# Loading k, q and v of the second step over the POOL queue, in one line with the weights

## The chip, the cores and the metric

The kernel runs on one core of a Trainium2 chip. The metric is the device time of one execution in microseconds (us); lower is better.

## The reference

There are two parts, one after the other. The first is gated linear attention with 4 batches, 8 heads, 768 positions and head size 48: with f = sigmoid(f_logit), at each position the 48 x 48 state of a head becomes `f * state + outer(k, v)`, and the output is `q @ state`. The second takes x, the outputs in rows of 8 x 48 = 384 (3072 rows), through a feed-forward net (FFN):

```
out = (relu(x @ w_gate) * (x @ w_val)) @ w_out     # 384 -> 1536 -> 384
```

Inputs and output are float32.

## The kernel before

**Steps and work items.** The sequence is cut into 6 steps of 128 positions. A work item is one step of one batch (all 8 heads, 4 pairs of heads), so there are 24. For an item, f goes through exp and ln on ACT, is summed along the step by a matmul with a triangle (L583; step 0: L482), and gives decay factors; k and q are multiplied with them into `hats` (L603, L606 on POOL; step 0: L509 on POOL for k and on DVE for q); TensorE transposes these (L616; step 0: L519), forms scores (L639), DVE masks them (L645), and TensorE forms the outputs from the scores and v (L667 for step 0, L678 later) and from the state (L674). The state is advanced by L719 and the lines after it. POOL casts v to bf16 into `vpad` first (L559). The outputs go as `xT` to the FFN.

**FFN.** `ffn_hidden` forms one of 12 slices of 128 hidden columns: a gate and a value matmul group (L767), relu on ACT (L774), and the product on DVE (L778). `ffn_out` multiplies the 12 slices with `wo` (L790), ACT copies the result out (L810), SP stores it (L813). For step 0 the hidden groups run in the order: slices 0 to 3 of batches 0 and 1, the same slices of batches 2 and 3, then slices 4 to 7 of batches 0 and 1, and so on; a chain named "ffn" keeps them in that order on TensorE.

**Loads.** Each load of f, k, q or v takes one batch (step 0) or two batches (384 KB, later steps). It is cut in runs of 192 bytes, 2048 of them for two batches; f, k and q of step 0 use runs of 384 bytes. SP issues all of these in one line (L400). The weights are float32 in memory and are cast to bf16 by the DMA; POOL issues them in one line (L420), in three slices each: wg0, wv0 to wg2, wv2, and wo0 to wo2. The list `early` gives the order for steps 0 and 1. Buffers of the inputs are three deep (`NL`).

**How two queues are kept apart.** In `early`, an item of one queue is tied to an item of the other that is `lag` planned microseconds of transfer behind it. For SP's loads this is a true dependency (a wait for the landing). For a weight it is `paced`, except for the three slices of wo, which truly wait for the landing of f, k and q of step 1 (`wo_after`).

**The plan.** `Plan.schedule` runs all operations through a model of the five engines and of the DMA (`occ`, `lat`, `prio`, `flow`, `late`), always taking the operation that can start first; ties go to the lower `prio`. The order found is the program order of each engine. `Plan.needs` then emits the waits, and leaves out two kinds of ties:

```
                if how in ("order", "pace"):
                    continue
```

So a paced operation has its place in the program order, worked out with planned times, but no wait on the chip. While TensorE would be idle in the plan before the first FFN group, it gets matmuls on zeros (L456). The first FFN group ends these.

Of the kernel before, what the change touches and what calls it, by code (L numbers as in the profile page):

```python
# [8 lines left out]
BF16 = mybir.dt.bfloat16  # L9
# [34 lines left out]
class Plan:  # L44
# [4 lines left out]
    def __init__(self, limits):  # L49
        self.ops = []  # L50
        self.limits = limits
        self.settled, self.margin = 0.0, {}

# [41 lines left out]
    def schedule(self, banks):  # L95
# [14 lines left out]
        left = len(self.ops)  # L110
        flow_free = 0.0

# [8 lines left out]
        while left:  # L121
# [17 lines left out]
            e = op.eng  # L139
# [14 lines left out]
            if op.flow is not None:  # L154
                backlog = max(flow_free - op.end, 0.0)
                flow_free = op.end + backlog + op.flow
                op.end += op.flow + op.late + (min(backlog, op.flow) if op.ring == "own" else backlog)
            free[e] = at + op.occ
# [70 lines left out]
def bass_hgrn2_outer__then__ffn_reglu_kernel(  # L229
# [12 lines left out]
             "q0.2.3 q0.3.4 v0.2.3 v0.3.4 wg0 wv0 wg1 wv1 wg2 wv2 f1.0.2 k1.0.2 q1.0.2 v1.0.2 wo0 wo1 "  # L242
             "wo2 f1.2.4 k1.2.4 q1.2.4 v1.2.4").split()
    lag = 4.0
    first_xbar_qk = 4
    flight = 3
    WP = 0
# [5 lines left out]
    n_tiled = 1  # L253
    first_xbar_x = 3
    load_batches = 2
    hat_engines = ['DVE', 'POOL']
    STORE = 'SP'
    TAIL = [0, 256, 384]
    groups = [(0,0,4,1),(1,0,2,0),(1,2,4,0),(2,0,4,0),(3,0,4,0),(4,0,4,0),(5,0,4,0)]
    B, H, S, D = q.shape  # L260
    C = 128
# [8 lines left out]

    VSTEP, SSTEP = 112, 96
    VW, SW = NP * VSTEP, NP * SSTEP
# [16 lines left out]
    NV = 4  # L289
    vpad = [sb(f"vpad{i}", [128, VW], BF16) for i in range(NV)]  # L290
    st = [[sb(f"st{b}_{i}", [128, SW], BF16) for i in range(2)] for b in range(B)]
# [28 lines left out]
    pl = Plan({"bc": 1, "tp": 1, "s": 4, "y": 1, "kv": 1, "f": 4, "w": 1})  # L320
    pl.settled, pl.margin = 40.0, {"PE": 0.5, "SP": 0.6}
    add = pl.add
    gp, ve, sc, te, sy = nc.gpsimd, nc.vector, nc.scalar, nc.tensor, nc.sync
# [41 lines left out]
    for i in range(NH):  # L365
        zero("DVE", ve, hats[i][:], f"hats{i}", 1024, -8)
    for i in range(NV):
        zero("POOL", gp, vpad[i][:], f"vpad{i}", VW, -7)
    for i in range(NA):
# [14 lines left out]
    srcs = {"f": f_logit, "k": k, "q": q, "v": v}  # L384

    def load(n, c, b0, b1, after=(), paced=(), eng="SP"):
        last = tails.get("load" + eng)
        e = sy if eng == "SP" else sc
        t = ld[n][c % NL]
        src = bass.AP(tensor=srcs[n].tensor, offset=b0 * H * S * D + c * C * D,  # L390
                      ap=[[D, C], [S * D, (b1 - b0) * H], [1, D]])
        dst = t[:, b0:b1, :, :].rearrange("p b h d -> p (b h) d")
        flow = 1.0 * (b1 - b0)
        if c == 0 and n != "v":
            u = b0 % 2
            src = bass.AP(tensor=srcs[n].tensor, offset=b0 * H * S * D, ap=[[2 * D, 64], [S * D, H], [1, 2 * D]])
            dst = t[64 * u:64 * u + 64, b0 - u:b0 - u + 2, :, :].rearrange("p b h d -> p (b h d)").rearrange(
                "p (h x) -> p h x", h=H)
            flow = 0.82
        op = add(eng, lambda: e.dma_start(dst, src), [], [f"{n}{c % NL}_{b}" for b in range(b0, b1)],  # L400
                 occ=(0.8 if eng == "SP" else 0.3) * (b1 - b0) * (0.8 if c == 0 else 1), lat=2.0 if c == 0 else 0.9, prio=c * 100 - 150 * (eng != "SP"), after=after,
                 follows=[last] if last else [], paced=paced)
        tails["load" + eng] = op
        dma(op, f"{n}{c % NL}_{b0}{b1}", flow, (6.0 if (c, n, b0) == (1, "v", 0) else 2.0) if c else 0.8)
        return op
# [4 lines left out]
    def load_w(nm, s, after, landed=()):  # L410
        if nm == "wo":
            src = bass.AP(tensor=w_out.tensor, offset=s * WJ * 128 * DM,
                          ap=[[DM, 128], [128 * DM, WJ], [1, DM]])
            dst = wo[:, s * WJ:(s + 1) * WJ, :]
        else:
            src = bass.AP(tensor=wsrc[nm].tensor, offset=s * WJ * 128,
                          ap=[[DFF, 128], [128 * DFF, NK], [1, WJ * 128]])
            dst = (wg if nm == "wg" else wv)[:, :, s * WJ * 128:(s + 1) * WJ * 128]
        last = tails.get("load_w")
        op = add("POOL", lambda: gp.dma_start(dst, src), [], [f"{nm}{s}"], occ=0.8, lat=1.0, prio=WP, paced=after,  # L420
                 after=landed, follows=[last] if last else [])
        tails["load_w"] = op
        dma(op, f"{nm}{s}", 6.3 / wsteps)
        return op


    done, first_of = [], {}
    wo_after = ['f', 'k', 'q']
    for item in early:
        weight = item[0] == "w"  # L430
        cost, need = 0.0, []
        for other, flow, op in reversed(done):
# [3 lines left out]
            cost += flow  # L436
        if weight:
            landed = [first_of[wo_after[int(item[2:])]]] if item[:2] == "wo" else []
            op = load_w(item[:2], int(item[2:]), [] if landed else need, landed)
# [107 lines left out]
    def attention(c, b):  # L547
# [5 lines left out]
        xi = c % NX  # L553
        fin, kin, qin, vin = (ld[n][li] for n in "fkqv")

        qk_key = [f"qkT{qi}_0", f"qkT{qi}_1"]
        vp = vpad[vi]
        vout = bass.AP(tensor=vp, offset=0, ap=[[VW, 128], [VSTEP, NP], [64, 2], [1, D]])
        add("POOL", lambda: gp.tensor_copy(vout, vin[:, b, :, :].rearrange("p (n j) d -> p n j d", j=2)), [f"v{li}_{b}", f"vpad{vi}"], [f"v_{vi}"],  # L559
            prio=P + 3, occ=0.15 + HD / 1200.0 * 1.1, lat=0.2)  # L560
# [7 lines left out]
        else:  # L568
# [27 lines left out]
            if c < NC - 1:  # L596
# [11 lines left out]
                [f"q{li}_{b}", f"expq{ei}", f"hats{hi}"], [f"hq{hi}"], prio=P + 2, occ=0.95, lat=0.2)  # L608
            if c < first_xbar_qk:
                tp = Bank("tp")  # L610
# [71 lines left out]
        if c < n_tiled:  # L682
            chain("intra", "PE", intra, qk_key + [f"v_{vi}", f"vpad{vi}", f"ptm{mi}_0", f"ptm{mi}_1"]
                  + (s_key if c else []), [y], occ=0.1 + (0.8 if c else 0.5), lat=PE_L, prio=P + 7, opens=[y])
# [3 lines left out]
        else:  # L688
# [4 lines left out]
                **act_t(HD))  # L693
            if c < first_xbar_x:
                xp = Bank("tp")
# [17 lines left out]
        if c < NC - 1:  # L713
# [3 lines left out]
            def state():  # L717
                for p in range(NP):
                    mm = te.matmul(kv.ap[:, p * 96:(p + 1) * 96],  # L719
                                   khat[:, p * 128:(p + 1) * 128],  # L720
                                   bass.AP(tensor=vp, offset=p * VSTEP, ap=[[VW, 128], [64, 2], [1, D]]))
                return mm
# [58 lines left out]
    def ffn_out(g, *bs):  # L781
# [26 lines left out]
        for b, n0, n1, o in parts:  # L808
# [6 lines left out]
            dma(op, f"osb{oi}_{n0}", 0.45 * (n1 - n0) / DM)  # L815

    first_stores = [tails["loadSP"]] if '0' == "1" else []
    OJ = 4
# [3 lines left out]
    pend = []  # L822
    loads = [op for weight, flow, op in done if not weight]
    len0 = 0
    for c in range(NC):
        for b in range(0, B, load_batches):
            for n in "fkqv":
                if c > max(int(x.split(".")[0]) for x in sent):
                    if load_engine == "SP":
# [105 lines left out]
```

## Time and profile before

| | us |
|---|---|
| median of 3 runs | 198.84 (198.35 to 201.0) |
| the profiled execution | 199.44 |
| its span in the profile | 197.3 |
| PE busy in it | 190.8 |
| DVE, ACT, POOL busy | 108.9, 115.9, 77.1 |

The profile is of one execution. PE is TensorE's matmuls, PEld its weight loads, POOL is GpSimd, SP the engine that issues most DMAs; a trailing q means an engine's queue of instructions. A line such as `24.60 0.41 PE L667 MATMUL ... x16` gives start, duration, engine, source line and how many instructions were merged; a bracket at its end tells how long the engine was idle before it and what ended that. The trace also has a record of each DMA packet with its queue, size, start and duration; where packet rates or landings are given, they are counted from these records (a landing is the last of the 16 semaphore packets that end a DMA).

### The profile page before, as it was taken

How to read it: one execution, taken by the hardware profiler on the slowest of the kernel's cores; microseconds unless marked ns; L12 is line 12 of the kernel's file. 1: busy time of each engine (PE TensorE's matmuls, PEld its weight loads, DVE VectorE, ACT ScalarE, POOL GpSimd, SP SyncE). 2: the span in 40 equal slices, each digit the busy share in tenths (PEclk: the TensorE clock that was granted, in tenths of full speed). 3: DMA queues.
4: the chain of work that ended last, by engine and by line, in shares of the span. 5: the costliest groups of instructions: out<-in, count | busy, mean ns of one | idle time of the engine just before them, and what ended most of it. 6: DMA issues, size and time to landing. Idle time of an engine off the chain costs nothing.

```text
span 197.3 us, 4555 instructions
## 1 busy us (share of the span) xinstructions
PE 190.8 (97%) x1804; PEld 125.5 (64%) x1819; DVE 108.9 (55%) x212; ACT 115.9 (59%) x264; POOL 77.1 (39%) x111
## 2 busy tenths in 40 slices
PE   7999899988999999999999999999999999999995
PEld 5777688856788687866565555554554555544564
DVE  7269675575098959586956562832645433442300
ACT  2975866905879495868668577386334433344312
POOL 5188302553567593949483744604500000000000
PEclk9999999999999999999999999999999999999999
DMA  4999999999998999899997996988951310111113
GB/s 122 234 224 193 181 212 204 201 207 234 250 240 177 195 196 204 176 194 199 133 205 155 232 186 138 203 194 170 150 133 40 47 50 26 40 43 40 40 40 120
DMA packets 114100, 30.70 MB, mean 156 GB/s; under 512 B 107040, under 2 KB 114080, under 8 KB 114080
## 3 DMA queue, kind: packets, MB, share of 16 engines
q1 hardware_dynamic: 110096, 26.88, 67.6%
q0 software_dynamic: 3984, 3.54, 11.6%
q8 instruction: 14, 0.23, 0.5%
q14 instruction: 6, 0.05, 0.1%
HBM read 25.95 MB, written 4.72 MB: 155 GB/s over the span
## 4 chain that ended last, share of the span: by engine, by line
PE 82%; DMA 6%; ACT 3%; SPq 2%; DVE 2%; POOL 2%; issue 1%
PE ps L767 43%; PE ps L790 23%; DMA wo<-in_moe_w_out_dram 4%; PE ps L639 3%; DMA q_in<-in_q_dram 2%; SPq L400 2%; PE ps L616 2%; PE ps L678 2%; PE ps L719 2%; PE ps L674 2%; PE ps L456 1%; PE ps L583 1%; ACT relu L774 1%; PE ps L519 1%; DVE hats L509 1%
## 5 line engine op out<-in xcount | busy, mean ns | idle before, releaser
L778 DVE TENSOR_TENSOR gT<-relu,ps 128x256 bf16<-128x256 bf16 (+1 forms) x96 | 52.1, 551 | 61.7 <-PE ps L767 40.9
L767 PE MATMUL ps<-xT,wv 128*128 128x256 bf16 (+1 forms) x285 | 61.8, 325 | 0.2
L774 ACT ACTIVATE relu<-ps 128x256 bf16<-128x256 f32 (+1 forms) x96 | 46.4, 491 | 25.4 <-PE ps L767 24.4
L767 PE MATMUL ps<-xT,wg 128*128 128x256 bf16 (+1 forms) x276 | 59.9, 323 | 0.5
L790 PE MATMUL ps<-wo,gT 128*128 128x384 bf16 (+2 forms) x300 | 52.2, 319 | 1.2 <-DMA wo<-in_moe_w_out_dram 1.2
L790 PEld LDWEIGHTS ps<-wo,gT 128*128 128x128 bf16 x300 | 27.9, 98 | 19.2 <-DMA wo<-in_moe_w_out_dram 1.6
L767 PEld LDWEIGHTS ps<-xT,wv 128*128 128x128 bf16 x288 | 26.7, 98 | 16.1
L767 PEld LDWEIGHTS ps<-xT,wg 128*128 128x128 bf16 x288 | 26.6, 98 | 14.8
L645 DVE TENSOR_TENSOR ptm<-ps,tri 128x512 bf16<-128x512 f32 x48 | 30.5, 683 | 4.4 <-PE ps L639 4.2
L810 ACT ACTIVATE osb<-ps 128x384 f32<-128x384 f32 (+2 forms) x25 | 11.8, 477 | 32.9 <-PE ps L790 32.9
L603 POOL TENSOR_TENSOR hats<-k_in,expo 128x384 bf16<-128x384 f32 x20 | 20.0, 998 | 20.9 <-ACT expo L592 20.9
L735 POOL TENSOR_TENSOR st<-ssum,dec 128x384 bf16<-128x384 f32 x16 | 13.2, 829 | 21.5 <-DVE ssum L733 21.4
L606 POOL TENSOR_TENSOR hats<-q_in,expo 128x384 bf16<-128x384 f32 x20 | 19.9, 1000 | 2.0 <-DMA q_in<-in_q_dram 2.0
L456 PE MATMUL ps<-zeros 128*128 128x256 bf16 x91 | 14.2, 316 | 1.1 <-DVE zeros L360 1.1
L592 ACT ACTIVATE expo<-ps 128x384 f32<-128x384 f32 x20 | 9.8, 490 | 9.0 <-PE ps L585 7.3
L559 POOL CAST vpad<-v_in 128x384 bf16<-128x384 f32 x24 | 11.9, 512 | 1.9 <-DMA v_in<-in_v_dram 1.2
L692 ACT ACTIVATE xn<-ps 128x384 bf16<-128x384 f32 x20 | 9.9, 495 | 3.9 <-PE ps L678 3.9
L456 PEld LDWEIGHTS ps<-zeros 128*128 128x128 bf16 x91 | 9.8, 113 | 3.4 <-DVE zeros L360 1.1
L733 DVE TENSOR_TENSOR ssum<-ps,st 128x384 f32<-128x384 f32 x16 | 8.8, 549 | 2.8 <-PE ps L719 2.8
L594 ACT ACTIVATE expo<-ps 128x384 f32<-128x384 f32 x20 | 9.9, 497 | 0.0
L639 PE MATMUL ps<-qkT 48*128 48x128 bf16 x192 | 8.5, 218 | 0.6 <-ACT qkT L529 0.5
L639 PEld LDWEIGHTS ps<-qkT 48*128 48x128 bf16 x192 | 5.4, 94 | 5.0 <-issue 3.1
(71 smaller groups left out, 162.0 us busy)
## 6 DMA issues: line engine op xcount, KB each, us to landing
out_dram<-osb SPq DMA_DIRECT2D x23, 192.0 KB, 2.1
f_in<-in_f_logit_dram SPq DMA_DIRECT2D x10, 384.0 KB, 6.4
k_in<-in_k_dram SPq DMA_DIRECT2D x10, 384.0 KB, 5.5
q_in<-in_q_dram SPq DMA_DIRECT2D x10, 384.0 KB, 4.1
v_in<-in_v_dram SPq DMA_DIRECT2D x10, 384.0 KB, 5.3
wg<-in_moe_w_gate_dram POOLq DMA_DIRECT2D x3, 384.0 KB, 7.4
wv<-in_moe_w_val_dram POOLq DMA_DIRECT2D x3, 384.0 KB, 7.4
wo<-in_moe_w_out_dram POOLq DMA_DIRECT2D x3, 384.0 KB, 7.4
```

The source lines that it names most:

```text
L456: op = add("PE", lambda: te.matmul(cold.ap[:, 0:256], zeros[:, 0:128], zeros[:, :]), ["zeros"], [cold], occ=0.22 if i < 17 else 0.11, lat= ...
L559: add("POOL", lambda: gp.tensor_copy(vout, vin[:, b, :, :].rearrange("p (n j) d -> p n j d", j=2)), [f"v{li}_{b}", f"vpad{vi}"], [f"v_{vi} ...
L603: add("POOL", lambda: gp.tensor_tensor(hk, kin[:, b, :, :], ex[:, 1, :].rearrange("p (h d) -> p h d", h=H), ALU.mult), [f"k{li}_{b}", f"ex ...
L606: add("POOL", lambda: gp.tensor_tensor(hq, qin[:, b, :, :], ex[:, 0, :].rearrange("p (h d) -> p h d", h=H), ALU.mult), [f"q{li}_{b}", f"ex ...
L639: mm = te.matmul(s.ap[:, p * C:(p + 1) * C], qkT[qi][lo:lo + D, 1, p, :], qkT[qi][lo:lo + D, 0, p, :])
L645: add("DVE", lambda j=j, s=s: ve.tensor_tensor(ptm[mi][:, j, :, :], s.ap[:, :].rearrange("p (n t) -> p n t", n=NP), mask, ALU.mult), [s, " ...
L735: add("POOL", lambda: gp.tensor_tensor(t4(s_new), t4(tmp), rate, ALU.mult), [key] + dk, [f"S{b}_{c % 2}"], prio=P + 8, **pool_t(HD))
L767: mm = te.matmul(bank.ap[:, 0:n], wt[:, kt, j * 128:(j + 1) * 128], xT[xi][:, kt, n0:n1], start=(kt == 0), stop=(kt == NK - 1))
L774: add("ACT", lambda: sc.activation(relu[ri][:, 0:n], gate.ap[:, 0:n], AF.Relu), [gate], [f"relu{ri}"], prio=P, **act_t(n))
L778: add("DVE", lambda: ve.tensor_tensor(gT[gi][:, j, n0:n1], relu[ri][:, 0:n], val.ap[:, 0:n], ALU.mult), [val, f"relu{ri}"], [f"gT{gi}_{j}_ ...
L790: mm = te.matmul(o.ap[:, 0:n1 - n0], gT[gi][:, j, b * C:(b + 1) * C], wo[:, j, n0:n1], start=(j == 0), stop=(j == NJ - 1))
L810: add("ACT", lambda o=o, oi=oi, n0=n0, n1=n1: sc.activation(osb[oi][:, n0:n1], o.ap[:, 0:n1 - n0], AF.Copy), [o], [f"osb{oi}_{x}" for x in ...
```

## The change

The loads of k, q and v of step 1 are issued by POOL instead of SP, in one chain ("soft") with the weights. They are paced and have no wait. f of step 1 stays on SP, with a true tie as before. The slices of wo lose their waits and are paced like the other weights. `lag` becomes 6, and in `early` wo2 moves behind k of batches 2 and 3. The plan's model has two DMA flows, SP's and POOL's, that slow each other, in the place of one. `vpad` becomes one tensor with a pitch of 128 columns for a pair of heads instead of 112, zeroed by one memset of the gaps. Two thresholds count work items instead of steps. The core of the diff:

```diff
     early = ("f0.0.1 f0.1.2 f0.2.3 f0.3.4 k0.0.1 k0.1.2 q0.0.1 q0.1.2 v0.0.1 v0.1.2 k0.2.3 k0.3.4 "
              "q0.2.3 q0.3.4 v0.2.3 v0.3.4 wg0 wv0 wg1 wv1 wg2 wv2 f1.0.2 k1.0.2 q1.0.2 v1.0.2 wo0 wo1 "
-             "wo2 f1.2.4 k1.2.4 q1.2.4 v1.2.4").split()
-    lag = 4.0
-    first_xbar_qk = 4
+             "f1.2.4 k1.2.4 wo2 q1.2.4 v1.2.4").split()
+    lag = 6.0
+    first_xbar_qk = 16
...
-    first_xbar_x = 3
+    first_xbar_x = 12
...
+    SOFT = {1: "kqv"}
...
             if op.flow is not None:
-                backlog = max(flow_free - op.end, 0.0)
-                flow_free = op.end + backlog + op.flow
-                op.end += op.flow + op.late + (min(backlog, op.flow) if op.ring == "own" else backlog)
+                me, you = ("POOL", "SP") if e == "POOL" else ("SP", "POOL")
+                backlog = max(flow_free[me] - op.end, 0.0)
+                shared = min(max(flow_free[you] - op.end - backlog, 0.0), op.flow * self.share[me])
+                flow_free[me] = op.end + backlog + op.flow + shared
+                flow_free[you] += min(shared, op.flow) if shared else 0.0
+                op.end += op.flow + op.late + backlog + shared
...
+    pl.share = {"SP": 2.0, "POOL": 0.4}
...
-    for i in range(NV):
-        zero("POOL", gp, vpad[i][:], f"vpad{i}", VW, -7)
+    add("POOL", lambda: gp.memset(vpad[:, 0:B, :].rearrange("p b (h x) -> p (b h) x", x=64)[:, :, D:64], 0.0), [], ["vpad"],
+        occ=0.6, prio=-7)
...
+    def load_soft(n, c, b0, b1, paced):
+
+        last = tails.get("soft")
+        t = ld[n][c % NL]
+        src = bass.AP(tensor=srcs[n].tensor, offset=b0 * H * S * D + c * C * D, ap=[[D, C], [S * D, (b1 - b0) * H], [1, D]])
+        dst = t[:, b0:b1, :, :].rearrange("p b h d -> p (b h) d")
+        op = add("POOL", lambda: gp.dma_start(dst, src), [], [f"{n}{c % NL}_{b}" for b in range(b0, b1)],
+                 occ=1.25, lat=1.0, prio=WP + c * 160 - 160, paced=paced, follows=[last] if last else [])
+        tails["soft"] = op
+        dma(op, f"s{n}{c % NL}_{b0}{b1}", 0.75 * (b1 - b0), 2.0)
...
     def load(n, c, b0, b1, after=(), paced=(), eng="SP"):
+        if n in SOFT.get(c, ""):
+            return load_soft(n, c, b0, b1, list(after) + list(paced))
...
-        last = tails.get("load_w")
+        last = tails.get("soft")
...
-    wo_after = ['f', 'k', 'q']
+    wo_after = ['none']
     for item in early:
-        weight = item[0] == "w"
+        weight = item[0] == "w" or item[0] in SOFT.get(int(item[1]), "")
...
-        if weight:
-            landed = [first_of[wo_after[int(item[2:])]]] if item[:2] == "wo" else []
+        if item[0] == "w":
+            landed = [first_of[wo_after[int(item[2:])]]] if item[:2] == "wo" and wo_after != ["none"] else []
...
-            if c < first_xbar_qk:
+            if w < first_xbar_qk:
...
-            if c < first_xbar_x:
+            if w < first_xbar_x:
```

## The prediction

> **What bounds the kernel now.** I read the page first, then the windows of five microseconds, the PE waits, the chain of waits, and last the POOL and PE timelines of the first 50 us.
>
> ```profile
> PE 190.8 (97%) x1804; PEld 125.5 (64%) x1819; DVE 108.9 (55%) x212; ACT 115.9 (59%) x264; POOL 77.1 (39%) x111
> PEclk9999999999999999999999999999999999999999
> ```
>
> ```profile
> 40.00:45.00 5.00, 3.82 (x38) 2.23 (x35) 2.94 (x6) 0.00 (x0) 2.29 (x4) 1.00 1.27 212
> ...
> 180.00:197.30 17.30, 14.93 (x96) 8.78 (x94) 3.43 (x5) 5.01 (x11) 0.00 (x0) 1.00 0.19 68
> ```
>
> The first lines are the page's: PE is busy 190.8 of 197.3 us at full clock. The second are windows: PE, PEld, DVE, ACT, POOL busy, clock, DMA share, GB/s. Of the 6.5 us idle, 1.1 lie before the first matmul and 2.4 in the last window, after the last one. Some 3 us are left, and 1.2 of them are one hole between 40 and 45 us. A change of loads can win that hole, some tenths beside it, and whatever it gains in the start; it can lose much more.
>
> ```profile
> PE ps L790 <- DMA wo<-in_moe_w_out_dram: 1.2, 1, 1.2
> ```
>
> ```profile
> 36.65 0.95 POOL hats L603
> 37.60 7.41 DMA wo<-in_moe_w_out_dram
> 45.06 0.82 PE ps L790 x4
> ```
>
> These are the PE waits, and the chain in order of time (start, duration). The hole is the third slice of wo: POOL issues it at 37.60, because its wait is released late and a hats product stands in front of it, and it lands 7.41 us later.
>
> The start is the other place. Up to 20.4 us PE runs attention of step 0 and fillers on zeros (L456, 91 matmuls, 14.2 us). From then on it is busy with FFN 0 almost without a hole, so a delay there moves the end.
>
> ```profile
> 12.43 0.51 POOL L559 CAST vpad<-v_in 128x384 bf16<-128x384 f32 x1 [0.56 <-DMA k_in<-in_k_dram]
> 12.88 0.93 POOL L420 DMA_DIRECT2D wg<-in_moe_w_gate_dram  x1
> 13.99 1.95 POOL L509 TENSOR_TENSOR hats<-k_in,expo 128x384 bf16<-128x384 f32 x2 [0.18 <-DMA k_in<-in_k_dram]
> 15.89 0.80 POOL L420 DMA_DIRECT2D wv<-in_moe_w_val_dram  x1
> 17.56 0.50 POOL L559 CAST vpad<-v_in 128x384 bf16<-128x384 f32 x1 [0.86 <-DMA v_in<-in_v_dram]
> 18.00 0.78 POOL L420 DMA_DIRECT2D wg<-in_moe_w_gate_dram  x1
> ...
> 21.09 0.52 POOL L559 CAST vpad<-v_in 128x384 bf16<-128x384 f32 x1
> 31.82 0.78 POOL L420 DMA_DIRECT2D wo<-in_moe_w_out_dram  x1 [10.21 <-DMA f_in<-in_f_logit_dram]
> ```
>
> ```profile
> 24.60 0.41 PE L667 MATMUL ps<-ptm,vpad 128*32 128x128 bf16 x16
> ...
> 25.77 0.49 PE L767 MATMUL ps<-xT,wv 128*128 128x256 bf16 x3
> 26.10 0.49 PE L767 MATMUL ps<-xT,wg 128*128 128x256 bf16 x3
> ```
>
> Here are POOL's and PE's timelines (start, duration, line). The lines to hold on to are the casts at 17.56 and 21.09: they are v of batches 2 and 3. The cast of batch 3 stands behind the last four weight issues. Its user, the intra matmuls of batch 3, starts at 24.60 because its mask product on DVE ends at 24.28. xT of batch 3 is written by 25.55 (ACT, 25.06 + 0.49). At 26.10 FFN 0 starts on batches 2 and 3; the code fixes that order (slice 0 of batches 0-1, slice 0 of batches 2-3, then slice 1). From cast end to this start the way is 1.0 us (0.95 from intra to xT, and a hop), so the cast may end at 25.1 instead of 21.6 before PE loses anything.
>
> **What the skill says.** "DMA: Bandwidth & Descriptors", section Issuing engines are not separate DMA queues: all issuers share the same 16 engines and "interleave with each other". Its section Queues, rings and completion order says that an engine goes round robin between its queues by packets. The packet records of this trace agree: alone, SP's 192-byte packets run at 530 to 640 in half a microsecond; from 42.0 to 43.5, beside wo, SP gets 311 packets in 1.5 us and wo 282, about one for one, though a weight packet holds an engine 78 to 98 ns and SP's 15. A weight in flight thus cuts SP to about a fifth. "Perfetto Trace Analysis", section DMA Instruction — SWDGE (GPSIMD): the profiled interval of a POOL DMA is the writing of descriptors, not the transfer. The trace agrees (0.78 us of issue, 7.4 to landing). "DMA: Bandwidth & Descriptors", section Anatomy of one DMA, says of that writing that many descriptors can be emitted before their cost shows; the trace has 384 runs at 0.77 to 0.93 us and 512 at 0.74 to 0.80, and nothing near the 2048 runs of a k, q or v load.
>
> **The change, part by part.**
>
> Pacing on POOL is no wait on the chip: needs() leaves it out, so it only fixes POOL's program order, worked out with planned times. The rule reproduces the order seen above: step 0 loads are planned to end every 0.82 or 1.0 us (k of batch 2 at 12.8, v of batch 2 at 16.3, v of batch 3 at 17.3), a DMA has priority 0, the casts of batches 2 and 3 have 23 and 33, and a DMA ready at the same time goes first. With a lag of 6 the same rule gives: wg0 at v of batch 0 (11.0), ahead of the casts of batches 0 and 1; wv0 at 12.8; two hats; wg1 at 15.3; the cast of batch 2 at 16.3; and at 17.3, all tied to v of batch 3, wv1, wg2, wv2, k, q, v of step 1 for batches 0-1, and wo0. Only then the cast of batch 3. Seven issues stand in front of it where four stood.
>
> *Issue cost D of a soft load.* No row shows it. From below 0.78 (as a weight), from above 0.78 x 2048/512 = 3.1 (in proportion to runs). I take 1.25, the planner's own occ: its 0.8 for a weight and its 0.64 for a step 0 load are what the trace has (0.77 to 0.80; 0.61 to 0.66).
>
> *Earlier weights.* wg0 follows the hats that end at 11.1. Before, it was issued at 12.88, its first packet came at 15.41 and full flow at 16.0; so now full flow from about 14.1. By the packets, SP then still has some 190 packets of q of batch 3 and 2000 of v of batches 2 and 3. One for one against wg0 and wv0 (768 packets at some 180 per us, to 18.4), v of batch 2 has 400 left; in the short gap before wg1 flows (issued at 15.95, full flow some 2.8 later) and then beside it, it lands at about 19.3 instead of 16.3. Bounds: 17, if POOL's first packets come a microsecond later than I think, and 20.5 without that gap. POOL sees a landing about 1 us later: the cast of batch 2 at 20.3, ended 20.8.
>
> *The cast of batch 3.* 20.8 + 3 x 0.78 (wv1, wg2, wv2) + 3 x 1.25 + 0.78 (wo0) = 27.6; it ends at 28.1, and FFN on batches 2-3 starts at 29.1 instead of 26.10: PE loses 3.0 us. Nothing fills the hole: fillers end with the first FFN group, step 1 has no f yet, and slice 1 stands behind in the FFN chain.
>
> *wo without waits, and the 1.2 us hole.* From wv1 (issued 20.8, flowing at 23.3) the POOL ring holds wv1, wg2, wv2 (1.95 each, the distance of their landings before), k, q, v (2048 x 15 ns / 16 = 1.9 each), wo0, wo1 (2.1: 512 packets at the 240 per us seen from 35 to 36.5), k, wo2. That is 23.3 + 5.9 + 5.7 + 4.2 + 1.9 + 2.1 = 43.1, and about 46 with f's 3.8 us beside it, shared in part. So wo2 lands no earlier than before (44.7), but PE comes to it 3 us later (46.8), with v of step 1 there at 37 instead of 41.25. The hole goes: -1.24. If k, q, v cost more on the engines it is back, up to 1.2.
>
> *f on SP.* f of batches 0-1 now waits for wg1, not wv1, and is issued at about 21.5 instead of 26.15; squeezed beside wv1 to wv2 it lands at 30 to 31 (31.2 before): no gain for step 1. SP loses six issues (0.37 to 1.85 us each, off the path) and goes on to step 2 when k of batches 2-3 lands, about 43 to 45; its first load was issued at 49.22, and PE never waited for a later load. Nothing.
>
> *The second lot on POOL* (wo1, k, wo2, q, v: 2 x 0.78 + 3 x 1.25 = 5.3 us), tied to f's planned landing, goes ahead of the first hats of step 1, which are ready some 3 us after f: 2.3 us later at most. PE has FFN 0's hidden groups until about 42, hats were due at 36.65: covered. Without that cover 2.3.
>
> *The rest.* vpad's memsets (0.95 us) become one; POOL is idle 5.7 us behind them. The cast keeps its 384 columns, the matmuls their shapes. The two thresholds for transposes, now in work items (16 = 4 x 4, 12 = 3 x 4), fall where they fell. Order noise from the new flow model: -0.5 to +0.5.
>
> Sum: +3.0 - 1.24 = +1.8 us. The profiled execution took 199.44 (span 197.3 and 2.1 around it); it becomes 201.2. It lies 0.6 above the median of 198.84, so I forecast 198.84 + 1.8 = 200.6. Its own range is 198.9 to 202.8 (v of batch 2 between 17 and 20.5; D between 1 and 1.6). About 2% (4 us) is what a measurement of this kernel can tell from no change.
>
> **Rivals.**
>
> *The start is not delayed; the hole goes.* D near 0.78 and v of batch 2 at 17: the cast of batch 3 starts at 18.5 + 7 x 0.78 = 24.0, ends at 24.5, within the 25.1. Then -1.24 and some tenths: 196.8 to 197.6. For it: 384 and 512 runs cost the same. Against it: four times as many runs, and earlier weights against v.
>
> *Issue of 2048 runs is dear (the slower side).* POOL, between wv2 and the cast of batch 3. Each microsecond of D above 1.25 delays FFN 0 by 3. It is slower by over 2% from D = 1.25 + (4.0 - 1.8)/3 = 2.0; at 3.1 it gives 200.6 + 5.6 = 206.2. For it: descriptors are written by POOL, four times as many, and no row says what they cost. Against: the equal 384 and 512.
>
> *wo lands later still.* In the one line wo2 stands behind four loads; if they take 2.5 us each on the engines instead of 1.9, wo2 comes 2.4 later, a hole of about 1.6 instead of none: 202.2. It falls in the forecast's range.
>
> **How the numbers follow.** Forecast 0.45, of it 0.03 above 202.8. Start not delayed 0.32, of it 0.03 below 194.9 (PE gaining in the start besides, by FFN taking the place of fillers at 19). Dear issue 0.15. wo later 0.08. Faster 0.03, slower 0.15 + 0.03 = 0.18, same 0.79. For 8 in 10 the range reaches down to 196.4, through most of the first rival, and up to 204.5, through half of the dear issue.
>
> **What would show it.** Right: wg issued on POOL at about 11.1, the cast of batch 2 idle for v until about 20, soft issues of about 1.25, the cast of batch 3 at 27 or 28, and a PE wait at L667 of 3 us near 25 to 28, with none on wo at L790. Wrong: soft issues under 0.9 or over 2; a cast of batch 3 before 25; no wait at L667; a wait on wo that stays; or a new wait at L616 or L639 near 35 to 45, which would mean that step 1 is late.

## The result, and the profile after

The changed kernel takes 212.54 us (median of four runs, 211.76 to 213.47), against 199.0 us (198.35 to 201.0) for the kernel before on the same chip. The ratio is 1.066, with an interval of 1.057 to 1.076. The forecast was 200.6, with a range of 196.4 to 204.5 for 8 in 10, so hardly a change; it missed by 12 us. The profiled execution took 213.12 us, its span 211.1, which is 13.8 more than before.

First the page of the changed kernel: the busy times, the clock, and the DMA queues (packets, MB, share of 16 engines).

```profile
PE 195.7 (93%) x1815; PEld 127.6 (60%) x1815; DVE 109.2 (52%) x212; ACT 115.5 (55%) x264; POOL 83.4 (39%) x114
PEclk9999975999589999999999999999999999999999
q1 hardware_dynamic: 97712, 24.52, 56.5%
q0 software_dynamic: 4656, 5.90, 14.9%
```

PE's idle time rose from 6.5 to 15.4 us (+8.9), and its busy time from 190.8 to 195.7 (+4.9), with hardly more matmuls. So there are two kinds of loss: holes (stretches in which PE stands idle and waits), and slow work. The second line says where: the clock falls around slices 6 to 7 (26 to 37 us) and 11 to 12 (53 to 63 us). In the queues the six loads are seen to move: q1, SP's, had 110096 packets before and lost 12384; q0, POOL's, had 3984 and gained 672. So POOL moves the same bytes in an eighteenth of the packets.

The PE waits (total, times, longest):

```profile
PE ps L660 <- ACT relu L795: 5.0, 1, 5.0
PE ps L740 <- POOL vpad L580: 4.9, 1, 4.9
...
PE ps L788 <- ACT xT L706: 0.6, 1, 0.6
```

There is no wait on wo any more (L811 now, L790 before). The two long ones are seen in PE's timeline:

```profile
29.80 0.50 PE L740 MATMUL ps<-vpad,khn 128*128 128x96 bf16 x4 [4.90 <-POOL vpad L580]
...
31.45 0.82 PE L788 MATMUL ps<-xT,wg 128*128 128x256 bf16 x3 [0.60 <-ACT xT L706]
...
36.23 0.49 PE L788 MATMUL ps<-xT,wg 128*128 128x256 bf16 x3
...
47.86 0.81 PE L811 MATMUL ps<-wo,gT 128*128 128x384 bf16 x4
53.62 0.61 PE L660 MATMUL ps<-qkT 48*128 48x128 bf16 x8 [4.96 <-ACT relu L795]
...
55.79 2.72 PE L811 MATMUL ps<-wo,gT 128*128 128x384 bf16 x8
```

**Hole one** has two parts, which end at 29.80 and 31.45: 4.90 + 0.60 = 5.5 us. Its aftermath costs more: the first seven FFN groups behind it start 0.636 us apart (31.45 to 35.90), later ones 0.33 (36.23 and on). **Hole two** ends at 53.62 after 4.96 us, and the wo groups after it run at half rate too (2.72 us for eight). The windows of five microseconds (length, then PE, PEld, DVE, ACT, POOL busy, clock, DMA share, GB/s) show that behind the holes the clock is what falls, not the supply of work:

```profile
31.00:36.00 5.00, 4.55 (x22) 3.25 (x23) 1.26 (x3) 1.54 (x4) 3.67 (x4) 0.51 1.14 235
...
46.00:51.00 5.00, 2.67 (x29) 2.02 (x27) 1.61 (x3) 0.19 (x1) 1.13 (x2) 1.00 1.16 235
...
56.00:61.00 5.00, 5.00 (x40) 3.02 (x39) 2.13 (x5) 2.52 (x9) 3.27 (x4) 0.62 0.00 0
```

From 56 to 61 PE is busy all the time at a clock of 0.62. The middle window holds half of hole two: the DMA moves 235 GB/s there, near the most of any stretch (246 in one slice of the page), so it is not bandwidth that is short. What it moves first is needed later. POOL's timeline shows hole one's cause:

```profile
11.01 0.92 POOL L441 DMA_DIRECT2D wg<-in_moe_w_gate_dram  x1
...
22.21 0.50 POOL L580 CAST vpad<-v_in 128x384 bf16<-128x384 f32 x1 [5.64 <-DMA v_in<-in_v_dram]
22.66 0.78 POOL L441 DMA_DIRECT2D wv<-in_moe_w_val_dram  x1
...
24.98 1.18 POOL L397 DMA_DIRECT2D k_in<-in_k_dram  x1
26.16 1.17 POOL L397 DMA_DIRECT2D q_in<-in_q_dram  x1
27.30 1.17 POOL L397 DMA_DIRECT2D v_in<-in_v_dram  x1
28.44 0.80 POOL L441 DMA_DIRECT2D wo<-in_moe_w_out_dram  x1
29.19 0.55 POOL L580 CAST vpad<-v_in 128x384 bf16<-128x384 f32 x1
```

The cast of batch 2 waits until 22.21 for v, and seven issues stand between it and the cast of batch 3 at 29.19. Hole two's cause is on ACT: its timeline before (one line), its timeline now, and the chain of waits now.

```profile
48.10 0.84 ACT L573 ACTIVATE f_in<-f_in 128x768 f32<-128x768 f32 x1
```

```profile
45.80 0.38 ACT L795 ACTIVATE relu<-ps 128x256 bf16<-128x256 f32 x1 [0.27 <-PE ps L788]
52.37 0.84 ACT L594 ACTIVATE f_in<-f_in 128x768 f32<-128x768 f32 x1 [6.18 <-DMA f_in<-in_f_logit_dram]
53.12 0.37 ACT L795 ACTIVATE relu<-ps 128x256 bf16<-128x256 f32 x1
```

```profile
12.02 10.14 DMA v_in<-in_v_dram
...
24.98 10.66 DMA k_in<-in_k_dram
35.64 0.02 issue
35.66 16.68 DMA f_in<-in_f_logit_dram
52.34 0.02 issue
52.37 0.84 ACT f_in L594
53.21 0.28 ACT relu L795
```

At 46.2 ACT comes to the exp of f of batches 2 and 3 of step 1, and stands there for 6.18 us. The relu behind it in ACT's order has its input, but waits too, and TensorE needs a bank that this relu frees. Two things changed: f landed at 45.1 before and lands at 51.5 now, and ACT came to it at 48.1 before and comes at 46.2 now. The f load was issued by SP at 35.66, when k had landed, and was seen 16.68 us later. In the median of the whole run, a load of that size took 4.7 to 6.1 us.

**The packet records of the trace say why it took so long.** SP's runs of 192 bytes travel as one packet each, 2048 a load, about 15 ns on an engine. The same load issued by POOL goes in packets of 22 runs (4224 bytes) and 18 runs (3456), 96 a load, about 305 and 260 ns each. For the engines the sum is about equal (96 x 305 = 29.3 us at most, 2048 x 15 = 30.7 us, over 16 engines 1.8 and 1.9 us; k, q and v landed at 34.67, 36.53, 38.37). For a neighbour it isn't: when the engines take about one packet from each queue in turn, SP gets one run while POOL gets 22. Between 47 and 49 us POOL's queue moved 147 packets and SP's 169, some 80 a microsecond; once POOL's had drained, SP's moved 1020 to 1270 a microsecond. The 2048 packets of f were issued at 35.66, and between 39 and 49 us only some 1380 passed.

The large packets are not the whole delay. The first packet of this load ran only at 39.67, 4 us after the issue. Up to 46 us it then ran mostly beside the 768-byte packets of wo, at 150 to 190 packets a microsecond; large packets were in flight from 42.3 to 44.6 (k) and from 46.2 to 50.7 (q and v).

**The sum.** Holes +5.5 and +4.96, the wo hole -1.24. Half clock: the seven groups after hole one took 4.45 us instead of 7 x 0.328 = 2.30 (+2.15), the state and intra matmuls ahead of them about +0.4; after hole two, +2.76 (8.30 us from L660 to L721, against 5.54 for the same instructions in the experiment with fillers below). Together +14.5: +9.2 of holes and +5.3 of slow work, where the page has +8.9 and +4.9. The measured 13.8 is about 0.7 less, and FFN 0 did begin earlier (at 19.80 instead of 20.36, with 87 fillers instead of 91).

### The profile page after: what moved, and what is told of

It is laid out like the page before. It is cut to its first block, busy times and chain, and to the rows that moved or that the text cites. A ratio compares the mean times of both kernels' runs of the same rounds, so it can differ in the third digit from the quotient of the medians.

```text
span 211.1 us, 4577 instructions
## 1 busy us (share of the span) xinstructions
PE 195.7 (93%) x1815; PEld 127.6 (60%) x1815; DVE 109.2 (52%) x212; ACT 115.5 (55%) x264; POOL 83.4 (39%) x114
## 4 chain that ended last, share of the span: by engine, by line
PE 73%; DMA 18%; SPq 5%; POOL 1%; ACT 1%; issue 0%
PE ps L788 37%; PE ps L811 23%; DMA f_in<-in_f_logit_dram 8%; DMA k_in<-in_k_dram 5%; SPq L421 5%; DMA v_in<-in_v_dram 5%; PE ps L660 3%; PE ps L637 3%; PE ps L699 2%; PE ps L604 2%; PE ps L695 2%; PE ps L740 1%; POOL wv L441 1%; PE ps L721 1%; PE ps L606 1%
## 5 line engine op out<-in xcount | busy, mean ns | idle before, releaser
L788 PE MATMUL ps<-xT,wg 128*128 128x256 bf16 (+1 forms) x288 | 63.8, 331 | 0.6 <-ACT xT L706 0.6
L788 PE MATMUL ps<-xT,wv 128*128 128x256 bf16 (+1 forms) x288 | 63.6, 330 | 0.0
L811 PE MATMUL ps<-wo,gT 128*128 128x384 bf16 (+2 forms) x300 | 53.8, 325 | 0.0
L811 PEld LDWEIGHTS ps<-wo,gT 128*128 128x128 bf16 x300 | 28.1, 99 | 17.7 <-issue 1.0
L788 PEld LDWEIGHTS ps<-xT,wg 128*128 128x128 bf16 x288 | 27.3, 99 | 16.7 <-ACT xT L706 0.9
L666 DVE TENSOR_TENSOR ptm<-ps,tri 128x512 bf16<-128x512 f32 x48 | 31.1, 684 | 10.3 <-PE ps L660 10.3
L624 POOL TENSOR_TENSOR hats<-k_in,expo 128x384 bf16<-128x384 f32 x20 | 19.9, 996 | 33.7 <-ACT expo L613 33.7
L477 PE MATMUL ps<-zeros 128*128 128x256 bf16 x87 | 12.9, 305 | 1.1 <-DVE zeros L365 1.1
L613 ACT ACTIVATE expo<-ps 128x384 f32<-128x384 f32 x20 | 9.8, 491 | 6.8 <-PE ps L606 5.5
L660 PE MATMUL ps<-qkT 48*128 48x128 bf16 x192 | 8.8, 224 | 5.0 <-ACT relu L795 5.0
L594 ACT ACTIVATE f_in<-f_in 128x768 f32<-128x768 f32 x10 | 8.4, 841 | 6.2 <-DMA f_in<-in_f_logit_dram 6.2
L660 PEld LDWEIGHTS ps<-qkT 48*128 48x128 bf16 x192 | 5.7, 97 | 9.3 <-issue 7.2
L477 PEld LDWEIGHTS ps<-zeros 128*128 128x128 bf16 x87 | 9.0, 109 | 3.0 <-DVE zeros L365 1.1
L643 DVE COPY qkT<-ps 128x1024 bf16<-128x1024 bf16 x12 | 8.2, 687 | 3.5 <-PE ps L637 3.4
```

The lines of the kernel that those rows point to most:

```text
L477: op = add("PE", lambda: te.matmul(cold.ap[:, 0:256], zeros[:, 0:128], zeros[:, :]), ["zeros"], [cold], occ=0.22 if i < 17 else 0.11, lat= ...
L624: add("POOL", lambda: gp.tensor_tensor(hk, kin[:, b, :, :], ex[:, 1, :].rearrange("p (h d) -> p h d", h=H), ALU.mult), [f"k{li}_{b}", f"ex ...
L660: mm = te.matmul(s.ap[:, p * C:(p + 1) * C], qkT[qi][lo:lo + D, 1, p, :], qkT[qi][lo:lo + D, 0, p, :])
L666: add("DVE", lambda j=j, s=s: ve.tensor_tensor(ptm[mi][:, j, :, :], s.ap[:, :].rearrange("p (n t) -> p n t", n=NP), mask, ALU.mult), [s, " ...
L788: mm = te.matmul(bank.ap[:, 0:n], wt[:, kt, j * 128:(j + 1) * 128], xT[xi][:, kt, n0:n1], start=(kt == 0), stop=(kt == NK - 1))
L811: mm = te.matmul(o.ap[:, 0:n1 - n0], gT[gi][:, j, b * C:(b + 1) * C], wo[:, j, n0:n1], start=(j == 0), stop=(j == NJ - 1))
```

## The experiments

The edits are against the changed kernel unless "before" is named. Ratios are to the kernel before, timed on the same chip.

**1. The cast of batch 3 ahead of the soft issues.**

```diff
-                 occ=1.25, lat=1.0, prio=WP + c * 160 - 160, paced=paced, ...
+                 occ=1.25, lat=1.0, prio=WP + c * 160 - 120, paced=paced, ...
```

> After, with the priority of the soft loads lowered, so that POOL casts v of batch 3 before it issues k, q, v of step 1 and wo0 (same loads, same queues). Theory (two holes, the second ended by the landing of f of batches 2-3 of step 1 near 52 us, because one 192-byte packet of SP passes for each 4 KB packet of POOL): the cast runs at 25.0 instead of 29.2, FFN 0 starts on batches 2-3 near 27 instead of 31.5, but f still lands at 52 to 53, so that the second hole grows by what the first loses; time 209 to 213. Rival (the late cast is the loss): both shrink, time near 205.

Measured: 212.73 us, ratio 1.064 (1.050 to 1.078), the same as without the edit. The cast of batch 3 starts at 26.80 instead of 29.19 and hole one shrinks from 5.5 to 1.7 us (1.1 and 0.6; even so the clock is halved behind it, from 29.2 to 32.6). The PE waits show where the gain went:

```profile
PE ps L660 <- ACT relu L795: 8.9, 1, 8.9
```

Hole two grew from 5.0 to 8.9 us: it ends when ACT has seen f (53.4; 52.4 without the edit), whatever the rest does. So hole one is made by the place of the cast, as predicted, and costs nothing while hole two stands.

**2. The old lag for wg and wv, the new one for the rest.**

```diff
-            if cost >= lag and other != weight:
+            if cost >= (4.0 if item[:2] in ("wg", "wv") else lag) and other != weight:
```

> After, with the lag of 4 kept for the six gate and value slices only, so that wg0 is issued behind the casts of batches 0 and 1 again. Theory (wg0 two microseconds earlier holds back v of batch 2, and POOL stands still at its cast): the cast of batch 2 runs at 17.6 instead of 22.2, that of batch 3 near 24.6 instead of 29.2, the first hole falls from 5.5 to under 1 us; the second hole stays or grows, as f's landing moves less than that; time 208 to 212. Rival (the soft issues alone make the first hole): the cast of batch 2 stays after 20.

Measured: 212.53 us, ratio 1.063 (1.051 to 1.075). Casts of batches 2 and 3 at 17.65 and 25.66, and of hole one 0.3 us are left: the lag is what made v late. But now f of batches 0 and 1 is the load that is held up. It was issued at 24.25 and landed 20.3 us later, at 44.56, and ACT and PE stood for it:

```profile
44.88 0.84 ACT L594 ACTIVATE f_in<-f_in 128x768 f32<-128x768 f32 x1 [11.89 <-DMA f_in<-in_f_logit_dram]
```

```profile
PE ps L604 <- ACT bneg L597: 11.6, 1, 11.6
```

With k, q and v issued 3.5 us earlier (21.45 instead of 24.98), f came to stand beside them entirely. So the delay is not tied to one load; what SP carried beside POOL's line paid in both kernels.

**3. f of batches 2 and 3 placed earlier in the order.**

```diff
-             ... wv2 f1.0.2 k1.0.2 q1.0.2 v1.0.2 wo0 wo1 f1.2.4 k1.2.4 wo2 q1.2.4 v1.2.4
+             ... wv2 f1.0.2 f1.2.4 k1.0.2 q1.0.2 v1.0.2 wo0 wo1 k1.2.4 wo2 q1.2.4 v1.2.4
```

> After, with f of batches 2-3 of step 1 moved ahead of k in the order, so that SP issues it when a value slice has landed (near 31 to 32) and not when k has landed (35.7). Theory (POOL's packets starve SP's queue): issuing it 4 us earlier does little, it stands behind f of batches 0-1 in a queue that moves 20 to 190 packets per us, and it lands at 47 to 52; time 207 to 212. Rival (the late issue is the cause): it lands within 7 us of its issue, near 39, the second hole is gone; time 204 or less.

Measured: 206.32 us, ratio 1.032 (1.025 to 1.039). f was issued at 29.84 and landed at 43.32, 13.5 us later. The theory had its landing at 47 to 52 and a time of 207 to 212, the rival had less than 7 us from issue and 204 or less; both fell between. ACT took it without a wait, and hole two is gone:

```profile
43.77 0.83 ACT L594 ACTIVATE f_in<-f_in 128x768 f32<-128x768 f32 x1
```

Hole one stays (4.6 + 0.6). The edit did more than was meant: the plan also put wo1 and the second lot of k, q and v behind the first hats, so POOL issued them at 43.6 to 48.7 and left the DMA to f in between. The 6.2 us that came back (212.5 - 206.3) are a little less than what hole two and its half clock had cost (5.0 + 2.8); that SP would have been held up just as long with the second lot in its old place was not seen here.

**4. k, q and v back on SP, all else as changed.**

```diff
-    SOFT = {1: "kqv"}
+    SOFT = {}
```

> After, with k, q and v of step 1 on SP again, all else as changed (lag 6, wo without waits, early weights, vpad, flow model). Theory (the soft loads make the cast of batch 3 late and starve f): no packets of 4 KB on POOL's queue, the cast of batch 3 at 25.0, a first hole of about 1 us, f of batches 2-3 in line on SP, landing near 46; time 200 to 206. Rival (early weights and wo without waits are to blame): time 209 or more.

Measured: 207.75 us, ratio 1.039 (1.029 to 1.049), above the theory's band and below the rival's. Both long holes go, but v of batch 2 is still late (its cast at 23.86: the lag of 6 makes it so, not the soft loads), and four holes of 3.1, 1.4, 0.6 and 2.5 us are left, with 3.4 us of half clock behind the first and the last. So the move of the loads is worth 4.8 us of the loss here, and the rest of the change 8 (207.75 - 199.73, the kernel before on this chip).

**5. The edits of 2 and 4 together.**

```diff
-    SOFT = {1: "kqv"}
+    SOFT = {}
...
-            if cost >= lag and other != weight:
+            if cost >= (4.0 if item[:2] in ("wg", "wv") else lag) and other != weight:
```

> After, with both suspects undone: lag 4 for the gate and value slices, and k, q and v of step 1 on SP. What stays changed is wo without waits, lag 6 elsewhere, vpad and the flow model. Theory (early weights and soft loads carry the loss): the cast of batch 2 at 17.6, that of batch 3 near 21.5, no first hole, no packets of 4 KB; what is left is f of step 1 held back by wo0 and wo1, which now go ahead of it (landing near 35 instead of 31), and a hole of up to 3 us for it or for wo2; time 198 to 203. Rival (the rest of the change, its order of PE and ACT, costs by itself): 205 or more.

Measured: 204.58 us, ratio 1.022 (1.011 to 1.033), between the theory's band and the rival's. The casts are back at 17.66 and 21.20. One long hole of 4.0 us is left: f of batches 0 and 1 was issued at 24.81 and landed at 36.5, and ACT waited for it with relus behind.

```profile
37.60 0.84 ACT L594 ACTIVATE f_in<-f_in 128x768 f32<-128x768 f32 x1 [4.26 <-DMA f_in<-in_f_logit_dram]
```

Experiment 2 differs from this one by the edit of `SOFT` alone. Beside weights this f took 11.7 us, with k, q and v in POOL's line as well 20.3: 8.6 us of its delay come with the soft loads, the rest does not. With 2 and 4 this makes a square: the lag costs 3.2 us without the soft loads (207.75 - 204.58) and nothing with them (212.54 - 212.53); the soft loads cost 8 us with the old lag and 4.8 with the new. The losses overlap, so no part's price can be read from one undone edit. And 5 us are lost with both undone. (The kernel before took 199.73 on the chip of 4 and 199.34 on that of 5.)

**6. Fillers in hole two.** 45 matmuls on zeros ahead of the first wo group keep TensorE awake through the hole; they replace idle time and change nothing else.

```diff
+                for i in range(45 if (g, b, s) == (0, 0, 0) else 0):
+                    te.matmul(o.ap[:, 0:256], zeros[:, 0:128], zeros[:, :])
```

> After, with 45 matmuls on zeros (4.8 us at full clock) put on TensorE ahead of the first wo group, where it is about to stand still for 5 us at 48.7. They write a bank that the next matmul starts anew; the useful work is the same. Theory (after a hole TensorE runs at half clock for some us, 3.0 us lost after the second hole): the wait shrinks to under 1 us, the groups after it run at 0.16 us for 128x384 instead of 0.32, the time falls by 2.5 to 3.5, to 209 to 210. Rival (the clock drop does not come from the hole): time unchanged.

Measured: span 208.7 instead of 211.1 in the profiled execution (210.77 us); a second run took 218.89, at a mean clock of 0.969 instead of 0.984, for a reason that no trace shows, so no ratio is given. PE's timeline is the answer, and its longest wait:

```profile
48.36 5.08 PE L811 MATMUL ps<-zeros 128*128 128x256 bf16 x45
...
55.24 1.46 PE L813 MATMUL ps<-wo,gT 128*128 128x384 bf16 x8
```

```profile
PE ps L740 <- POOL vpad L580: 5.7, 1, 5.7
```

The eight wo matmuls take 1.46 us instead of 2.72, and from L660 to L721 the work takes 5.54 us instead of 8.30. Hole one was there, and 0.8 us longer (5.7 + 0.6); in all the span is 2.4 us shorter. So the half clock after a hole is a loss of its own, 2.76 us for a hole of 5, and filling the hole wins that part alone.

**7. Kernel before, wo without waits.**

```diff
-    wo_after = ['f', 'k', 'q']
+    wo_after = ['none']
```

> Before, with the slices of wo paced instead of waiting, nothing else. POOL's order then has wo0 behind the cast of batch 3, wo1 behind the first hats product of step 1, wo2 behind the fourth. Theory (transfers are bound by the engines, an earlier wo0 pushes f back, and wo2 is now behind four hats): f of step 1 lands near 33 instead of 31.2, wo2 is issued near 41 to 42 instead of 37.6, the hole of 1.2 us grows to 3 or 4; time 201 to 203. Rival (the waits are what costs): the hole closes, time 198.

Measured: 201.98 us, ratio 1.011 (1.006 to 1.016). wo0 was issued at 21.41 instead of 31.82, and landed beside f; many small holes (the largest 0.9 us) came for the one of 1.2; the hole of 3 to 4 us that was expected did not. The step taken alone costs 2.6 us: it puts a load that is needed late beside one that is needed early.

**8. Kernel before, wo2 waiting for k instead of q.**

```diff
-    wo_after = ['f', 'k', 'q']
+    wo_after = ['f', 'f', 'k']
```

> Before, with the three slices of wo waiting for f, f and k of step 1 instead of f, k and q; POOL's order then has all three ahead of the first hats product. Theory (the hole of 1.2 us is wo2's late issue): wo2 is issued near 34 instead of 37.6 and lands near 41.5 instead of 44.7, the hole closes; time 0.8 to 1.3 below before, if v of step 1, pushed back to 43, opens none of its own. Rival (engines bound): the hole moves to v or to f of batches 2-3; time as before or up to 2 above.

Measured: 199.35 us in 18 runs, ratio 1.002 (0.9996 to 1.004). wo2 landed at 42.05 instead of 44.7 and the hole was gone: no PE hole over 1 us but that at the start. The profiled execution had a span of 195.8, 1.5 less than before; its 197.88 us is the lowest of the 18, and the median didn't move. Why a hole that is gone in the trace isn't gone in the median stays open.

**9. The soft loads, with the old lag, order and waits of wo.**

```diff
-             "f1.2.4 k1.2.4 wo2 q1.2.4 v1.2.4").split()
-    lag = 6.0
+             "wo2 f1.2.4 k1.2.4 q1.2.4 v1.2.4").split()
+    lag = 4.0
...
-    wo_after = ['none']
+    wo_after = ['f', 'k', 'q']
```

> After with everything but the soft loads put back: lag 4 throughout, the old order, wo waiting for f, k and q. Theory (soft loads hold back f on SP, as one small packet passes for each large one): no first hole (cast of batch 3 near 25), f of batches 0-1 lands at 36 to 38 instead of 31.2, wo0, which waits for it, is issued near 38 and the slices land at 42 to 47; a hole of 2 to 5 us before a wo group or a step 1 group; time 202 to 206. Rival (soft loads alone do no harm, it takes the unwaited wo beside them): 200 or less.

Measured: 206.29 us, ratio 1.036 (1.031 to 1.040), a little above the expected band. f of batches 0 and 1 landed at 37.63 (31.2 before), which holds wo0 back to 38.26; f of batches 2 and 3 landed at 53.7. No hole is longer than 1.65 us and the clock stays at 1.0, and yet the many small ones add up: PE is idle for 12.8 us instead of 6.5. So 6.5 us (206.29 - 199.74) are lost with none of the other steps that were suspected, apart from the plan's new flow model, which this kernel has as well.

**10. f in the same line too.** With the edits of 1 and 2:

```diff
-    SOFT = {1: "kqv"}
+    SOFT = {1: "fkqv"}
...
-             "f1.2.4 k1.2.4 wo2 q1.2.4 v1.2.4").split()
+             "wo2 f1.2.4 k1.2.4 q1.2.4 v1.2.4").split()
```

> After, with f of step 1 on POOL too, the cast of batch 3 ahead of the soft loads, lag 4 for gate and value slices, wo2 before f of batches 2-3: one line for every load of step 1 and all weights, without waits. Theory (loss comes from f alone on the other queue and from the late casts, and a soft load holds the engines as long as SP's, 1.85 us against 1.9): landings in line, f near 31.5, wo0 39, wo2 43.5, f of batches 2-3 at 45; no hole over 0.5 us, TensorE at full clock; time as before, 197 to 200. Rival (POOL's issues, 8 x 1.2 us, or large packets do harm of their own): 202 or more.

Measured: 198.89 us in 20 runs, against 199.74 for the kernel before in 23; ratio 0.997 (0.994 to 0.999). From the page, POOL's timeline and ACT's:

```profile
PE 189.2 (96%) x1801; PEld 123.7 (63%) x1815; DVE 109.1 (56%) x212; ACT 116.2 (59%) x264; POOL 85.8 (44%) x116
...
q0 software_dynamic: 4880, 6.69, 18.5%
```

```profile
20.73 0.52 POOL L580 CAST vpad<-v_in 128x384 bf16<-128x384 f32 x1
21.18 1.18 POOL L397 DMA_DIRECT2D f_in<-in_f_logit_dram  x1
22.36 1.17 POOL L397 DMA_DIRECT2D k_in<-in_k_dram  x1
```

```profile
44.45 0.84 ACT L594 ACTIVATE f_in<-f_in 128x768 f32<-128x768 f32 x1 [0.71 <-DMA f_in<-in_f_logit_dram]
```

Everything that step 1 needs now lands in the order of its issue, one after the other: f 31.07, k 32.88, q 34.71, v 36.40, wo 38.33 to 42.02, f of batches 2 and 3 at 43.50. ACT waits 0.71 us for that f instead of 6.18, PE not at all, and the clock is 1.0. Against the changed kernel, only two PE holes of 0.8 and 0.7 us, at the first weights, are new. A loss of 13.5 us turns into a gain of 0.8. From experiment 2, which has 1.063, this differs by f's two loads, the place of the cast and of wo2; the hole of 11.6 us that went was f's. It is the fastest of all, by little.

**11 and 12. What is left with every load back on its queue.** Loads on SP, the old lag for wg and wv (the edit of 2), and wo waiting again. Of the change they keep the new flow model, the place of wo2 in the list, the lag of 6 for step 1 and the layout of `vpad`. The change also cuts the plan's allowance for the landing of v of step 1 on SP from 6.0 to 0.8 us. That means nothing while POOL loads this v, but 4, 5 and 11 have it; 12 puts it back.

```diff
-    SOFT = {1: "kqv"}
+    SOFT = {}
...
-    wo_after = ['none']
+    wo_after = ['f', 'k', 'q']
```

```diff
-        dma(op, ..., flow, (0.8 if (c, n, b0) == (1, "v", 0) else 2.0) if c else 0.8)
+        dma(op, ..., flow, (6.0 if (c, n, b0) == (1, "v", 0) else 2.0) if c else 0.8)
```

> After, with k, q, v on SP, lag 4 for gate and value slices, and wo waiting for f, k and q again. What stays changed: lag 6 for SP's loads of step 1, wo2 one place later in the order, vpad, the flow model. Theory (the rest costs nothing): f lands near 31 to 33, the hole before wo2 is 1 to 3 us (wo2 is issued behind one hats product more or less), time 198 to 201. Rival (the flow model's order costs by itself): 202 or more.

> The kernel of e11 with one planned number put back: the allowance for v of step 1 on SP is 6.0 us late again instead of 0.8. POOL then casts v of step 1 behind all four hats products, as before the change, and not ahead of the second pair. Theory (e11's hole of 3.9 us is that cast, standing in POOL's order for a v that lands near 42.7): the hole before the state matmul goes, what is left is at most the old hole of 1.2 us before wo; time 198.5 to 200.5. Rival (lag 6 or the two-flow model costs by itself): 202 or more.

Measured: 203.79 us, ratio 1.023 (1.018 to 1.029), and 204.54 us, ratio 1.025 (1.016 to 1.034). Both missed the time of the kernel before that my theory wanted; both lie in the rival's range. POOL's timeline of 11 and ACT's of 12:

```profile
43.13 0.50 POOL L580 CAST vpad<-v_in 128x384 bf16<-128x384 f32 x1 [4.28 <-DMA v_in<-in_v_dram]
```

```profile
45.83 0.84 ACT L594 ACTIVATE f_in<-f_in 128x768 f32<-128x768 f32 x1 [4.96 <-DMA f_in<-in_f_logit_dram]
```

In 11 POOL stands at a cast that the plan had put ahead of hats that were ready. In 12 that is gone and ACT stands at f of batches 2 and 3. f landed there at 45.33, as before (45.1); the plan had it at 40.1, where the old model had planned 47.4. So the transfer isn't late: the order written for ACT asks for it too early, and ACT, which keeps that order, then stands. 4 to 5 us are lost without a single load moved.

Which of the things kept makes the plan so early? The planner can be run alone, without the chip. With the flow model of before put into 12 it has f at 41.1, only 1 us later. With the new flow model, but the lag of 4 throughout and wo2 in its old place, it has f at 45.1, where the chip has it. So most of it is the tie and not the flow model: before, f of batches 2 and 3 waited for wo0, and with lag and place as kept in 12 it waits for wv2, which comes five loads earlier. This is worked out from the plan; neither was put back alone on the chip. Experiments 4 and 5 kept these things too, so they don't show what the change costs without the move and nothing else.

In the changed kernel the two meet: the plan has f at 39.7, and it lands at 51.5. In experiment 10 plan and chip agree, 43.9 and 43.5, and nothing stands.

## Why the prediction was wrong, point by point

**What held.** POOL's order was predicted instruction for instruction: wg0 at 11.01 (11.1 predicted), the idle time for v of batch 2, seven issues ahead of the cast of batch 3. The soft issue was taken at 1.25 us and is 1.17 to 1.24; so the rival in which it is dear, which carried most of the chance of slower, was false, and the slower side came by another way. The cast of batch 3 ended at 29.7, later than the 25.1 that PE could bear, so the rival in which the start is not delayed was false too. wo2 landed at 47.4 (about 46 predicted), PE didn't wait for it: -1.24 as in the sum. k, q and v took 1.85 us each (1.9 predicted, by luck: the sum took SP's packets, and the large ones hold the engines about as long).

**A term too small: hole one, +3.0 predicted, +5.5 measured.** The mechanism was right. v of batch 2 was put at POOL's view at 20.3, and was seen at 22.21, outside the bounds. Of the 32 semaphore packets of the two v loads half were in by 19.9 and the last came at 23.4: the count of packets gave a mean over 16 engines, and a landing is the slowest of them. The cast of batch 3 then came 1.6 us later than worked out, FFN 2.3: from the cast's end to FFN it took 1.7 us instead of 1.0, at half clock and with the state matmuls (L740) ahead of the intra matmuls (L688).

**The step that failed: "f on SP ... no gain for step 1 ... Nothing."** It costed f of batches 0 and 1 only, and that at the weights' rate: 30 to 31 predicted, landed at 37.2, which PE's work hid. It didn't follow f of batches 2 and 3 to its reader at all, the load that made hole two, +4.96. (Its last sign of being wrong, a new wait at L639, did come: L660 now, from 48.7 to 53.6, later than the 35 to 45 that it gave.) The rule that it quoted, round robin by packets, fits the counts; what was missing was the packet's size, and that wo, without its waits, would stand beside this f. The engine sum (2048 x 15 ns / 16) was carried over to the moved loads as if they kept SP's small packets. The Trainium skill, "DMA: Bandwidth & Descriptors", section SWDGE vs HWDGE vs iDMA, names the packet as the engine's "context-switching boundary", at up to 4096 bytes preferably and up to 64 descriptors. The trace has 4224 bytes and 22 runs. Had I asked how many of the 192-byte runs could share a packet on POOL's queue, an estimate could have followed: with 305 ns for POOL's packet and 15 for SP's, SP gets some 16 engines / 0.32 us = 50 packets a microsecond (20 to 85 measured), against 150 to 190 beside weights. That one packet alternates with one is read from counts in the traces; no run changed the packet's size alone.

**A term left out: what a hole does to the clock, +5.3.** The Trainium skill, "TensorE: Matmul & The Clock Gate", section What's actually happening, says that the array falls to half rate after an idle window of about 3.4 us and takes about as long of busy time to come back. The trace agrees in part. After the holes of 4.9 and 5.0 us the clock is halved until 6.1 and 6.2 us past their ends, and holes of 3.5 to 4 us (experiments 12, 5 and 11) brought the mean clock to 0.991, 0.992 and 0.983. But less was enough: half rate also followed holes of 3.1 and 2.5 us (experiment 4), and, in experiment 1, 3.4 us (25.8 to 29.2) in which PE was busy for 1.5 us without a hole over 1.2. In experiment 9, with none over 1.65, it did not come. So the length of a single hole doesn't decide. The sum took a hole at its length; the holes of 5 us cost about half as much again.

**A term mis-sized: "Order noise from the new flow model: -0.5 to +0.5."** Experiments 11 and 12 lose 4 to 5 us to orders of the plan with no load moved. In 12 it is, by the plan's own figures, chiefly the tie of f, which the lag and the list set, and not the flow model. The prediction followed planned times on POOL, where they set the order of issues, but not on ACT, where they set the order of waits.

**What is the cause?** Three things, which overlap: SP's loads are held up by what POOL moves beside them (2 against 5, and 10), the plan has ACT ask for f earlier than it comes (12), and the lag makes v late (2, and 4 against 5). The lag by itself costs 1.6% (207.75 over 204.58), what is left of the plan 2.5% (12), the soft loads with the old lag, order and waits 3.6% (9), and taking one away hands the loss to the next (1, 2). Not tried: soft loads beside SP's f with a plan that has f's true landing time.

## What to carry to other kernels

Before moving a load to another queue, ask for the packet size on both. Here a queue of 192-byte packets got 20 to 85 packets a microsecond beside packets of 4224 bytes, 150 to 190 beside packets of 768 and 1024, and 1020 to 1270 alone; what the step needed first should not have been left on it. Where the order of an engine is fixed beforehand, compare the planned landings with the trace, since one load planned too early stops all that stands behind it. Follow every load of the step to its first reader. And price what follows a hole on TensorE: here, holes of 5 us cost half as much again, and shorter ones close together also halved the clock.

## What the runs showed of the hardware

Not expected: POOL's DMAs of 192-byte runs are packed by 22 into one packet (4224 bytes, 305 ns), while its casting weight loads aren't packed (one run of 1024 or 768 bytes a packet, 98 or 78 ns). Issuing 2048 runs takes POOL 1.17 to 1.24 us, 384 to 512 runs 0.74 to 0.82 (the first of all 0.92), so four to five times the runs cost only half as much again. And a 384 KB load that SP moves in 4 to 6 us took 16.7 and 20.6 us until it was seen, beside such packets and the weights'. TensorE's clock was halved for 3.4 us after a stretch with no hole over 1.2 us (experiment 1).
